# Block 0's in-projections: planning the products of three pairs of heads before the fourth pair's x is there

## The chip, the cores and the metric

The kernel runs on one core of a Trainium2 chip, with its TensorE (PE in the profile), VectorE (DVE), ScalarE (ACT), GpSimd (POOL) and the queue of SyncE (SP) that issues most of the DMAs. The metric is the device time of one execution in microseconds; the median of three runs of the kernel before is 1342.89 us.

## What is computed

Attention over 8 batches of 8 heads, 576 positions and 64 channels, in which every score below the row's maximum less tau is dropped, and then a gated unit (a GLU) over all 4608 tokens. The reference, cut:

```
scores = scale * (q @ k.T)
scores = where(scores >= max(scores) - tau, scores, -1e9)
attn   = exp(scores - max(scores)); attn /= sum(attn) + 1e-9
x      = (attn @ v)            # per token: 8 heads x 64 = 512 channels
gate   = 1 / (1 + exp(-(x @ w_gate)))      # 512 -> 1536
out    = (gate * (x @ w_val)) @ w_out      # 1536 -> 512
```

The gate's weights are drawn large, so the products are made with split operands: each float32 is a high and a low part, and a product is the sum of three matmuls (high x high, high x low, low x high).

## The kernel before

**Attention.** A `Visit` is one pair of heads of one batch: 4 visits a batch, 32 in all. A visit has 9 tiles of 128 queries. For each tile TensorE makes the scores (tile `s`, L653 in the first four visits, L661 after them), VectorE takes their maximum (L668), ScalarE the exponential (L682), VectorE cuts and sums (L685), TensorE transposes the result (tiles `tp`, `lk`, L767 and L780), ScalarE copies that to SBUF (`pt`, L718), and TensorE multiplies by v (`av`, L803). The result of a visit is `xf`. In three visits of four the division by the row sums comes late, on `xf`, by way of a small DMA round trip and a GpSimd multiply (`late_normalise`, L713); the visit of the fourth pair (`hp == 3`) divides before its transposes (L756).

**x.** `split_x` turns `xf` into `x`, with a high part by ScalarE (L813) and a low part by GpSimd (L815). The four pairs of a batch are the four 128-row pieces of the 512 channels of x.

**In-projections.** `in_units` handles a block of 512 tokens (here: blocks 0, 1 and 2; the others are worked two at a time by another function). For each of 12 pieces f of the 1536 columns and each of i = 0 (gate) and i = 1 (value), one sum is made in a PSUM bank `m`: 4 pairs c times 3 matmuls, twelve products (L863), in the order of c. They are given to the planner in twos. Twelve products with what follows are a unit. After a gate's sum ScalarE takes the tanh (`th`, L877); after a value's sum VectorE multiplies (L881), and the halves go to `g`. The first operation of a value's sum also reserves `g[f]` and `th`.

**Weights.** `convert` brings the weights from 64-bit pairs to high and low parts, with ScalarE (L487, L508), VectorE (L490, L496) and GpSimd (L483, L514). It is spread over attention. Its intermediate `wb` takes a PSUM bank from L487 to L496. The first 16 weights of the in-projections stay in buffers of `g` (at most ten of the twelve until these are needed), the next 8 in buffers of `w`; block 0 reads all 24 from there. A copy goes to DRAM (L519) for the later blocks.

**The planner.** Each piece of work is an operation with an engine, an estimated cost, a key, and the buffers that it reads and writes. `Plan.run` plays the whole kernel through with these costs. An engine that is free takes the ready operation with the smallest key whose buffers have room (`room`). The order so found is the order in which instructions are written out, and each engine works through its instructions in that order. On the chip an instruction waits for the data that it itself reads. Attention has keys of 0 to some 340, the products of the unit have keys from 1e6 on, in order: TensorE takes a product only where no operation of attention is ready and has room. From the second visit of batch 1 on, attention is held to the pace of the units (`held_by`).

**PSUM.** There are eight banks. Before the first product is given out, scores have three buffers of two banks each (0-1, 2-3, 4-5), and banks 6 and 7 serve everything else (`tp`, `lk`, `av` and the conversions' `wb`). The operation with key 1e6, the first product, switches that (`started`): scores keep two buffers, and banks 4 and 5 join 6 and 7 when they are free. While attention lasts, sums may hold two of these four, attention two and conversions one:

```
            if cls == "conv":
                return 1
            if cls == "att":
                return 2 if active["moe"] else 3
            return 2 if active["att"] else 4
```

The rule that the change touches is in `in_units`: which pairs of x an operation of two products (j and j + 1) is said to read.

```
cs = range(ND) if ms[j + step - 1][0] >= FIRST_PAIRS else range(FIRST_PAIRS)
```

`ms[e][0]` is the pair of product e (0 to 3), `step` is 2, and ND is 4.

Of the kernel before, what the change touches and what calls it, by code (L numbers as in the profile page):

```python
# [281 lines left out]
def LATE(b, hp):  # L282
    return hp != 3

FIRST_PAIRS = 4
KD_COST = 1.2

TWOS = ((3, 4), (5, 6), (7, 8))
# [27 lines left out]
def kernel(  # L316
# [528 lines left out]
    def in_units(blk, xs, g, c0, c1, c0x, weights):  # L845
# [5 lines left out]
        for f in [f + z for f in F1 for z in (0, 2)] if blk in SUMS_IN else range(NF):  # L851
            th = buf("t2", [P, W], F32, f"th{blk}_{f}_{c0}")
            for i in range(2):
# [4 lines left out]
                for j in range(0, 12, step):  # L858
# [9 lines left out]

                    cs = range(ND) if ms[j + step - 1][0] >= FIRST_PAIRS else range(FIRST_PAIRS)
                    xr = [xs[c] if part is None else (xs[c], (z, c0)) for c in cs for z in range(2)]  # L870
# [516 lines left out]
```

## Time and profile before

| | us |
|---|---|
| median of three runs | 1342.89 |
| fastest and slowest of them | 1341.32, 1348.61 |
| span of the profiled execution | 1340.2 |
| VectorE, ScalarE, GpSimd busy in it | 944.4, 727.8, 492.7 |
| first and last in-projection product of block 0 (L863, weights ws) | 98.1, 231.7 |
| first and last of blocks 1 and 2 (L863, weights wi) | 324.4, 766.4 |

The profile is of one execution, and its own time is given by its span, the time from the first to the last instruction. The runs' times also hold what lies around the span. The profile has views by stretch of time (busy time of each engine, number of instructions in brackets, granted TensorE clock, share and rate of DMA), timelines of single engines, and groups by line. In the latter, a row has the number of instructions, their shortest, median and longest duration in ns, and the first and last start in us. TensorE's weight loads are a row of their own (PEld) and run beside its matmuls.

### The profile page before, as it was taken

To read this page: it belongs to the slowest core of one execution; us is meant where nothing else is said; L and a number is where in the kernel's file an instruction comes from. 1 tells how busy PE (TensorE), PEld (TensorE's weight loads), DVE (VectorE), ACT (ScalarE), POOL (GpSimd) and SP (SyncE) were. 2 spreads that over 40 slices of the span, in tenths; PEclk is the share of its full clock that TensorE was granted. 3 is DMA by queue.
4 is the path that set the end of the run, shared out by engine and by line. 5 is a ranking of instruction groups with operands and counts; after the bars stand their busy time and mean duration, and the time that the engine had idled before them with its cause. 6 is when DMAs were issued, how large, how long until landed. Compare 5 with 4: busy or idle time off the path is not lost.

```text
span 1340.2 us, 23378 instructions
## 1 busy us (share of the span) xinstructions
PE 1314.8 (98%) x8292; PEld 1077.3 (80%) x8292; DVE 944.4 (70%) x1868; ACT 727.8 (54%) x1339; POOL 492.7 (37%) x474
## 2 busy tenths in 40 slices
PE   8889999999999999999999999999999999999998
PEld 5558887888888888888888888888888888888887
DVE  7888888777787776776777763556955569554594
ACT  8887777667767766666666652223522235322242
POOL 3576867724455363456464441110001010001100
PEclk9999999999999999999999999999999999999999
DMA  8889998999798888998988957656686566756563
GB/s 298 240 260 311 321 259 263 269 260 288 198 254 259 239 241 244 260 293 230 264 246 259 236 190 267 221 191 207 211 286 196 189 204 206 247 178 204 190 217 117
DMA packets 148115, 318.72 MB, mean 238 GB/s; under 512 B 28192, under 2 KB 56096, under 8 KB 148000
## 3 DMA queue, kind: packets, MB, share of 16 engines
q1 hardware_dynamic: 147856, 317.24, 78.3%
q8 instruction: 66, 1.08, 0.3%
q14 instruction: 49, 0.40, 0.1%
q10 hardware_dynamic: 144, 0.00, 0.0%
HBM read 211.16 MB, written 54.64 MB: 198 GB/s over the span
## 4 chain that ended last, share of the span: by engine, by line
PE 91%; DMA 4%; ACT 2%; POOL 1%; DVE 1%; issue 1%; SPq 0%; DVEq 0%; POOLq 0%; ACTq 0%
PE m L863 13%; PE qb L1105 11%; PE av L803 11%; PE s L661 8%; PE tp L767 8%; PE qc L1105 7%; PE qa L1105 7%; PE o L906 7%; PE rb L1170 5%; PE rc L1170 4%; PE ra L1170 4%; PE s_l L661 1%; PE tp_l L767 1%; PE s L653 1%; PE lk L780 1%
## 5 line engine op out<-in xcount | busy, mean ns | idle before, releaser
L668 DVE TENSOR_REDUCE st<-s 128x1 f32<-128x576 f32 x256 | 192.4, 753 | 83.2 <-PE s L661 76.0
L685 DVE SCALAR_TENSOR_TENSOR p<-s,st,p 128x576 f32<-128x576 f32 x256 | 206.5, 813 | 44.7 <-ACT p L682 39.4
L682 ACT ACTIVATE p<-s,st 128x576 f32<-128x576 f32 x256 | 191.1, 751 | 35.1 <-DVE st L668 34.4
L718 ACT COPY pt<-tp 128x512 f32<-128x512 f32 x256 | 149.4, 588 | 83.1 <-PE tp L767 79.1
L1018 POOL TENSOR_TENSOR gA<-gA 128x512 f32<-128x512 f32 x18 | 24.1, 1341 | 409.5 <-DVE gA L1084 409.5
L661 PE MATMUL s<-kd,qd 128*128 128x288 f32 x896 | 163.2, 306 | 2.6 <-DVE p_l L685 1.9
L863 PE MATMUL m<-x,wi 128*128 128x512 f32 x576 | 164.9, 405 | 0.0
L767 PE MATMUL tp<-ident,p 128*128 128x128 f32 x1024 | 155.4, 276 | 8.2 <-ACT pt L718 4.1
L767 PEld LDWEIGHTS tp<-ident,p 128*128 128x128 f32 x1024 | 119.8, 140 | 40.4 <-ACT pt L718 5.6
L661 PEld LDWEIGHTS s<-kd,qd 128*128 128x128 f32 x896 | 134.5, 189 | 13.4 <-DVE p_l L685 2.6
L803 PE MATMUL av<-pt,vs 128*64 128x256 f32 x1024 | 124.6, 385 | 0.8 <-ACT pt L718 0.8
L906 PE MATMUL o<-g,wo 128*128 128x512 f32 x432 | 120.4, 404 | 0.0
L1105 PE MATMUL qa<-xs_p,wa 128*128 128x512 f32 x432 | 109.4, 389 | 0.0
L1042 DVE TENSOR_TENSOR qu<-qb,qp 128x512 f32<-128x512 f32 x72 | 49.8, 692 | 82.5 <-PE qb L1105 71.2
L863 PEld LDWEIGHTS m<-x,wi 128*128 128x128 f32 x576 | 98.0, 189 | 12.0
L803 PEld LDWEIGHTS av<-pt,vs 128*64 128x64 f32 x1024 | 67.9, 136 | 48.5 <-issue 9.5
L1105 PEld LDWEIGHTS qa<-xs_p,wa 128*128 128x128 f32 x432 | 81.1, 188 | 16.8
L906 PEld LDWEIGHTS o<-g,wo 128*128 128x128 f32 x432 | 74.7, 189 | 10.0
L863 PE MATMUL m<-x,ws 128*128 128x512 f32 x288 | 78.5, 404 | 1.5 <-ACT pt L718 1.5
L887 POOL TENSOR_TENSOR g<-th,g 128x512 fp32r<-128x512 f32 x36 | 46.7, 1296 | 58.0 <-ACT g L885 57.8
L756 POOL TENSOR_SCALAR p<-p,zero_t,sm 128x576 f32<-128x576 f32 x64 | 56.5, 892 | 31.1 <-DVE sm L754 19.3
L1010 ACT CAST gs_p<-gA 128x512 fp32r<-128x512 f32 x54 | 32.8, 620 | 61.4 <-DVE gA L1084 23.0
(145 smaller groups left out, 2542.1 us busy)
## 6 DMA issues: line engine op xcount, KB each, us to landing
kd<-k SPq DMA_DIRECT2D x112, 320.0 KB
wi<-wid SPq DMA_DIRECT2D x48, 512.0 KB
wo<-wod SPq DMA_DIRECT2D x36, 512.0 KB
wa<-wid SPq DMA_DIRECT2D x36, 512.0 KB
ws<-sid SPq DMA_DIRECT2D x36, 512.0 KB
wt<-sid SPq DMA_DIRECT2D x36, 512.0 KB
wo_p<-sod SPq DMA_DIRECT2D x36, 512.0 KB
qd<-q SPq DMA_DIRECT2D x112, 128.0 KB
```

The costliest lines, as they stand in the source:

```text
L661: nc.tensor.matmul(s.ap[:, c, :HALF], st(), mv(slice(kc + c * HALF, kc + (c + 1) * HALF)), start=m == 0, stop=m == len(steps) - 1,)
L668: op("DVE", 0.76, key, lambda: nc.vector.tensor_reduce(out=st.ap[:, 0:1], in_=sv(), axis=AX.XY, op=ALU.max, negate=True), reads=[s], write ...
L682: op("ACT", 0.74, key, lambda: nc.scalar.activation(p(), sv(), AF.Exp, bias=st.ap[:, 0:1], scale=1.0), reads=[s, (st, 0)], writes=[(g.p, i)])
L685: op("DVE", 0.9, key, lambda: nc.vector.scalar_tensor_tensor(out=p(), in0=sv(), scalar=st.ap[:, 1:2], in1=p(), op0=ALU.is_ge, op1=ALU.mult ...
L718: return op("ACT", act(n), key, lambda: nc.scalar.copy(dst(), src.ap), reads=[src], writes=[part])
L756: op("POOL", 0.9, key, lambda i=i: nc.gpsimd.tensor_scalar(out=p.ap[:, i * S : (i + 1) * S], in0=p.ap[:, i * S : (i + 1) * S], scalar1=zer ...
L767: nc.tensor.matmul(tp.ap[:, c, :], self.p.ap[:, o + c * P : o + (c + 1) * P], ident, is_transpose=True, start=c == 0, stop=c == NJ - 1, sk ...
L803: nc.tensor.matmul(av.ap[h * D : (h + 1) * D, a:z], vis.vs.ap[:, j, h], m(h), start=i == 0, stop=i == len(ms) - 1, skip_group_check=True,)
L863: nc.tensor.matmul(m.ap, wv[:, a, c * P : (c + 1) * P], xs[c].ap[:, z, c0:c1], start=e == 0, stop=e == 11,)
L906: nc.tensor.matmul(acc.ap, wv[:, f, a], g[fg * ND + f].ap[:, z], start=(fg, f, a, z) == (0, 0, 0, 0), stop=(fg, f, a, z) == (NFG - 1, ND - ...
L1105: nc.tensor.matmul(acc.ap, wv[:, y, (2 * h + c) * P : (2 * h + c + 1) * P], xt[prod][c].get()[:, z], start=e == 0 and prod in FIRST, stop= ...
L1170: nc.tensor.matmul(acc.ap, w.ap[:, e, c, y], gt[prod][2 * g + c].get()[:, z], start=m == 0 and g == 0 and prod in FIRST, stop=m == 5 and g ...
```

## The change

One constant. With 4, every operation of two products is planned to read all four pairs of x. With 3, an operation whose later product belongs to one of the first three pairs is planned to read those three, and one whose later product belongs to the fourth is planned to read all four.

```diff
@@ -282,7 +282,7 @@
 def LATE(b, hp):
     return hp != 3
 
-FIRST_PAIRS = 4
+FIRST_PAIRS = 3
 KD_COST = 1.2
```

The instructions that are written out are the same; their order may differ.

## Prediction

> **What bounds the kernel now.** I read the page from the top: the shares of the engines, then the chain that ended last.
>
> ```profile
> span 1340.2 us, 23378 instructions
> PE 1314.8 (98%) x8292; PEld 1077.3 (80%) x8292; DVE 944.4 (70%) x1868; ACT 727.8 (54%) x1339; POOL 492.7 (37%) x474
> PE 91%; DMA 4%; ACT 2%; POOL 1%; DVE 1%; issue 1%; SPq 0%; DVEq 0%; POOLq 0%; ACTq 0%
> ```
>
> TensorE is busy for 1314.8 of 1340.2 us and is 91% of the last chain. An edit that leaves its matmuls as they are can only move the remaining 25.4 us. So the next view is the one that gives busy time by stretch, cut at the moments around the change: 79.84 (x of the third pair is complete), 98.13 (the first product of block 0 starts), 140, 800 (attention is over).
>
> ```profile
> core 0: us, PE busy (x) PEld busy (x) DVE busy (x) ACT busy (x) POOL busy (x), PEclk, DMA share, GB/s
> 0.00:79.84 79.84, 67.87 (x539) 43.04 (x540) 65.12 (x139) 65.75 (x125) 42.97 (x73) 1.00 0.81 266
> 79.84:98.13 18.29, 14.20 (x124) 10.21 (x122) 17.44 (x35) 15.85 (x31) 14.58 (x16) 1.00 0.84 256
> 98.13:140.00 41.87, 41.07 (x266) 33.88 (x267) 35.73 (x74) 32.17 (x62) 26.25 (x24) 1.00 1.02 306
> 140.00:800.00 660.00, 655.51 (x4969) 546.72 (x4968) 494.64 (x1125) 446.11 (x835) 355.46 (x324) 1.00 0.89 254
> 800.00:1325.00 525.00, 525.00 (x2353) 434.50 (x2352) 329.42 (x494) 167.88 (x289) 53.46 (x40) 1.00 0.65 212
> ```
>
> Idle TensorE time is length less busy time: 11.97 us before 79.84, then 4.09, 0.80, 4.49 and 0.00 us. From 98.13 on TensorE is the bound. In the 18.29 us before it is not: there VectorE is busy for 17.44 us. That stretch is the only place where the change can collect anything.
>
> Its two ends come from the timeline of GpSimd, whose L815 completes x of one pair, and its gaps from the timeline of TensorE (columns: start, length, what; in brackets the idle time before it).
>
> ```profile
> 78.57 1.27 POOL L815 TENSOR_TENSOR x<-xf,x 128x512 fp32r<-128x512 f32 x1
> 92.62 1.28 POOL L815 TENSOR_TENSOR x<-xf,x 128x512 fp32r<-128x512 f32 x1 [1.53 <-ACT x L813]
> ```
> ```profile
> 80.42 0.33 PE L780 MATMUL lk<-ident,p 128*128 128x128 f32 x1 [0.24 <-ACT pt L718]
> 81.01 0.78 PE L661 MATMUL s<-kd,qd 128*128 128x288 f32 x4 [0.26 <-DMA xp<-xf]
> ...
> 85.24 0.63 PE L767 MATMUL tp<-ident,p 128*128 128x128 f32 x4 [0.41 <-ACT xf L718]
> 86.63 0.63 PE L767 MATMUL tp<-ident,p 128*128 128x128 f32 x4 [0.77 <-ACT pt L718]
> ...
> 87.72 0.80 PE L661 MATMUL s<-kd,qd 128*128 128x288 f32 x4 [0.35 <-DVE p L685]
> ...
> 94.61 0.66 PE L767 MATMUL tp_l<-ident,p_l 128*128 128x128 f32 x4 [0.57 <-ACT pt L718]
> ...
> 96.80 0.65 PE L767 MATMUL tp<-ident,p 128*128 128x128 f32 x4 [0.65 <-ACT pl_l L718]
> 98.13 3.02 PE L863 MATMUL m<-x,ws 128*128 128x512 f32 x12 [0.68 <-ACT pt L718]
> ```
>
> x of the third pair is complete at 78.57 + 1.27 = 79.84 us, x of the fourth at 93.90 us, and the first product starts at 98.13 us. The eight gaps shown sum to 3.93 us.
>
> **The change, part by part.** It removes and adds no instruction. It changes one list of reads that the planner goes by. Products are planned in twos, and a two waits for all four pairs as soon as its second product belongs to the fourth. So of the twelve products of a sum the first eight, four twos, can go after the third pair; the ninth shares a two with the tenth and still waits. The rule stands for blocks 1 and 2 too, but there x is early:
>
> ```profile
> L863 PE MATMUL m<-x,wi x576: 387/393/486, 324.4 to 766.4; 128*128 128x512 f32 x192
> ...
> L815 POOL TENSOR_TENSOR x<-xf,x x4: 1279/1286/1290, 145.9 to 235.3; 128x512 fp32r<-128x512 f32 x4
> ```
>
> Block 1 multiplies from 324.4 us; its last x was split at 235.3 us. Nothing to win or lose there, and block 2's x is reloaded in the same way during the work before it. The first weights are not late either: their copies go out from 30.7 us on.
>
> ```profile
> L519 SPq DMA_DIRECT2D wid<-ws x11: 321/343/782, 30.7 to 104.0; - x11
> ```
>
> *How much can move.* Two sums may be open beside attention (the cap of two banks), so 2 x 8 = 16 products. Twelve took 3.02 us at 98.13, 0.252 us each: 16 x 0.252 = **4.03 us** of TensorE work. The stretch has 4.09 us idle, so it would just fit. It issues no DMA: weights of block 0 lie in SBUF. Nothing on SP's or GpSimd's queue is passed.
>
> *What of it lands in gaps.* A sum needs a PSUM bank, and until the first product has been given out, attention and weight conversion share two. So I let the first product start some us after 79.84 and count the gaps from 86.63 on: 0.77 + 0.35 + 0.57 + 0.65 + 0.68 = 3.02 us. Bounds: 0 (no bank, or the order doesn't change) and 4.03 us. I take **3.4 us**, between 3.02 and 3.93, the gaps from 80.42.
>
> *What it costs.* TensorE works in order, so a two (0.50 us) that has begun holds up scores and transposes behind it, and with them VectorE, which has only 18.29 - 17.44 = 0.85 us to spare, and so x of the fourth pair. Also, with the first product the planner takes the third scores buffer from attention and gives its two banks to the others. Both together are in the trace, in the next stretch (L685 has two records a tile):
>
> ```profile
> 79.84:98.13 18.29, 4.83 (x12) 1.00 0.84 256
> 98.13:140.00 41.87, 9.70 (x24) 1.00 1.02 306
> ```
> ```profile
> 98.13:140.00 41.87, 26.79 (x104) 18.52 (x104) 1.00 1.02 306
> ```
>
> The first fence is L685, the second the products of L863. Before 98.13 a tile takes 18.29 / 6 = 3.05 us, after it 41.87 / 12 = 3.49 us, with products on TensorE for 26.79 / 41.87 = 64% of the time. At worst the six tiles get that slower pace: 6 x 0.44 = 2.6 us. But the moved products are only 4.03 / 18.29 = 22% of the stretch, so I scale: 2.6 x 22 / 64 = **0.9 us**. Bounds 0 and 2.6. The second sum also reserves its output g and th at its first product; as the early weights are kept to ten of the twelve g buffers, one conversion may slip. It is off TensorE, and I cost it at nothing; were it on the chain, it would cost its place there, about 3 us (below).
>
> *Sum.* 3.4 - 0.9 = 2.5 us less. On the profiled span: 1340.2 - 2.5 = 1337.7 us. The median run, 1342.89, lies 2.7 us above the span (the fastest, 1341.32, 1.1 us), so I forecast 1342.9 - 2.5 = **1340.4 us**.
>
> [...]
>
> **The rivals.**
>
> *A. Nothing is collected.* The first product finds no free bank until about where it is now, or the delay of x eats the gain (3.0 - 2.6 = 0.4 us). For it: x of the fourth pair is ready at 93.90, yet the first product starts 4.23 us later. Against it: the gaps at 85 to 88 us are waits for a copy or for VectorE, in which the planner had nothing else to give to TensorE. Time: 1342.9 us less 0 to 0.4.
>
> *B. Slower: open sums sit on the banks.* The two half sums can't finish before the fourth pair's x, 14.06 us after the third's. If they take the two banks that attention and conversion use, these have to live on the pair that the third scores buffer leaves. While that buffer is still held, or if only one of the pair serves, conversion and transposes take turns. A conversion's hold on its bank:
>
> ```profile
> 83.63 0.66 ACT L487 ACTIVATE wb<-wr 128x512 f32<-128x512 f32 x1
> ```
> ```profile
> 86.25 0.69 DVE L496 SCALAR_TENSOR_TENSOR wa<-wr,wb 128x512 int32<-128x512 int32 x1
> 86.85 0.81 DVE L685 SCALAR_TENSOR_TENSOR p<-s,st,p 128x576 f32<-128x576 f32 x1
> ```
> ```profile
> 79.84:98.13 18.29, 3.27 (x5) 1.00 0.84 256
> ```
>
> That is 86.94 - 83.63 = 3.3 us, five times in the stretch (last fence, L487). Each conversion that attention has to sit out costs 3.3 us; the point from which B decides is one. A scores buffer can be held for 6.6 us (scores at 81.01, consumed at 87.66, the L685 above), so two may fall into the hand-over: 2 x 3.3 - 3.4 = 3.2 us slower, **1346 us**; all five, 13.1 us slower, 1356 us. The half of the sums that takes the freed pair instead speaks against it: then attention and conversion have two banks, as before.
> [...]
>
> *C. The order after it is dealt anew.* All of attention to 800 us is placed by the same planner, so a moved start moves everything behind it. From 98.13 to 800 TensorE idles 0.80 + 4.49 = 5.3 us. Another order can save all of that or double it: 1340.4 - 5.3 = 1335.1 to 1340.4 + 5.3 = 1345.7 us. From 800 to 1325 there is no idle time to change.
>
> **How the numbers follow.** Forecast 0.45 (alone: 1338.9, if all 4.03 us are won, to 1342.5), A 0.20, B 0.17, C 0.18. About 0.5%, 6.7 us, is what a measurement of this kernel can tell from no change; the three runs before spread over 7.3 us. Faster by more than that, below 1336.2, only the lucky end of C reaches, helped by the spread of runs: 0.09. Slower by more, above 1349.6: B from three conversions on, and the spread on top of C: 0.15. Within: 0.76. The range runs from C's lucky end, 1335, to 1349, between B's two conversions and its three (1342.9 + 9.9 - 3.4 = 1349.4).
>
> **What would show it.** Right: L863's first start falls from 98.1 to 80 to 88 us, with 16 products ahead of the fourth x split; idle TensorE time between 79.84 and some 99 us falls from 4.09 to under 2 us; the fourth x split ends at 93.9 to 96.5 us. A: first start above 93 us, or the split late by as much as was filled. B: longer gaps before tp and lk, with releasers of pt, wb or wa, and the split after 97 us. C: an unlike idle time from 98 to 800 us than 5.3. The forecast is wrong if TensorE waits in order for a product whose x isn't there, which would show as a gap ahead of L863 released by L815.

## The result and the profile after

The changed kernel takes 1354.51 us (median of 6 runs, 1349.72 to 1358.86) against 1343.55 us before (6 runs, 1341.32 to 1348.61). The ratio is 1.0078, with a 95% interval of 1.0053 to 1.0103: slower by 11.0 us, where 2.5 us less were forecast. The measured time lies above the range.

The page of the profile after, with the same rows as before:

```profile
span 1353.3 us, 23378 instructions
PE 1321.2 (98%) x8292; PEld 1078.2 (80%) x8292; DVE 944.6 (70%) x1868; ACT 727.2 (54%) x1339; POOL 494.5 (37%) x474
PE 88%; DMA 5%; ACT 2%; SPq 1%; POOL 1%; DVE 1%; issue 1%; ACTq 0%; POOLq 0%; DVEq 0%
```

The third row above carries the shares of the chain that ended last. The span is 13.1 us longer. Idle TensorE time is 1353.3 - 1321.2 = 32.1 us, 6.7 more than before; busy time is 6.4 us more, for the same 8292 matmuls. So there are two losses to find: gaps, and matmuls that take longer.

Busy time by stretch, cut where it was cut before:

```profile
0.00:79.84 79.84, 68.87 (x532) 43.27 (x532) 65.00 (x139) 64.58 (x122) 41.35 (x71) 0.98 0.81 264
79.84:98.13 18.29, 16.05 (x131) 12.25 (x131) 15.83 (x31) 14.06 (x28) 11.74 (x13) 1.00 0.75 218
98.13:140.00 41.87, 41.09 (x262) 34.09 (x263) 37.00 (x71) 35.00 (x68) 32.86 (x30) 1.00 0.99 328
140.00:800.00 660.00, 646.32 (x4888) 535.17 (x4887) 481.81 (x1105) 438.38 (x824) 345.37 (x313) 0.99 0.88 250
800.00:1325.00 525.00, 524.43 (x2377) 433.50 (x2376) 334.31 (x508) 170.72 (x295) 63.18 (x49) 1.00 0.65 213
```

In the stretch at which the change aims, idle TensorE time fell from 4.09 to 2.24 us. From 140 to 800 us it rose from 4.49 to 13.68 us. Nothing of the changed line runs there in a new way: blocks 1 and 2 had their x early.

The start of the products, in TensorE's timeline, and x of the third and fourth pair, in GpSimd's:

```profile
82.31 2.11 PE L863 MATMUL m<-x,ws 128*128 128x512 f32 x8 [0.16 <-ACT pt L718]
```
```profile
79.97 1.27 POOL L815 TENSOR_TENSOR x<-xf,x 128x512 fp32r<-128x512 f32 x1
96.58 1.29 POOL L815 TENSOR_TENSOR x<-xf,x 128x512 fp32r<-128x512 f32 x1 [6.26 <-ACT x L813]
```

The first product starts at 82.31 instead of 98.13 us. x of the fourth pair is complete at 97.87 instead of 93.90 us.

**Where the time goes.** Two stalls between 200 and 260 us. Each is a chain over several engines, so it is shown by one row of each engine's timeline. The first, from SP's, ScalarE's and TensorE's timeline:

```profile
205.11 1.05 SPq L523 DMA_DIRECT2D wod<-ws  x1
```
```profile
212.61 0.62 ACT L508 CAST ws<-wa 128x512 fp32r<-128x512 f32 x1 [4.76 <-DMA wod<-ws]
```
```profile
213.77 3.00 PE L803 MATMUL av<-pt,vs 128*64 128x256 f32 x16 [2.49 <-ACT pt L718]
216.55 1.07 PE L803 MATMUL av<-pl,vs 128*64 128x128 f32 x8
217.56 0.89 PE L863 MATMUL m<-x,ws 128*128 128x512 f32 x2
```

A converted weight `ws` is to go into a `w` buffer whose old content is on its way to DRAM (L523). ScalarE stands for 4.76 us until the store that SP issued at 205.11 us has landed, 7.4 us after it. Behind that instruction stand the copy of `pt` and two exponentials, and TensorE waits for the copy. The second stall, in the same order with GpSimd's timeline added:

```profile
232.57 0.56 SPq L989 DMA_DIRECT2D sod<-s_o  x1
233.42 0.55 SPq L1278 DMA_DIRECT2D xp<-xf  x1
234.06 1.20 SPq L989 DMA_DIRECT2D sod<-s_o  x1
235.31 6.86 SPq L841 DMA_DIRECT2D wo<-wod  x3
```
```profile
241.16 1.27 POOL L957 TENSOR_TENSOR s_o<-wo 128x512 f32<-128x512 f32 x1 [10.48 <-DMA sod<-s_o]
```
```profile
249.01 0.62 ACT L968 CAST s_o<-s_o 128x512 fp32r<-128x512 f32 x1 [4.45 <-POOL s_o L957]
249.53 0.58 ACT L718 COPY pt<-tp 128x512 f32<-128x512 f32 x1
```
```profile
245.58 0.63 PE L906 MATMUL o<-g,wo 128*128 128x512 f32 x2
250.17 1.12 PE L767 MATMUL tp<-ident,p 128*128 128x128 f32 x4 [3.96 <-ACT pt L718]
250.94 2.06 PE L906 MATMUL o<-g,wo 128*128 128x512 f32 x4
```

GpSimd prepares sums of output weights for the blocks that are worked two at a time (`out_sums`), in `w` buffers too. The next such sum waits 10.48 us for a buffer that is still being stored: by L989 at 232.57 us, and this store lands at 241.03 us. SP itself waits 5.2 us for the second store, the one of 234.06 us; the last of its three loads stands behind that, so the row of 6.86 us is mostly waiting (`SPq L841 <- DMA sod<-s_o: 5.2, 1, 5.2` in the view of SP's waits). Behind GpSimd's waiting instruction stand the low parts of two x and one g and four more steps of the sum; ScalarE's next step waits for those, the copy of `pt` stands behind that, and TensorE idles for 3.96 us. TensorE's releaser reads "ACT pt" in both stalls, but it is neither ScalarE nor its copy: one has to follow the queue back to the store.

After each gap the matmuls are slow: sixteen `av` take 3.00 us where the same group takes 1.95 us elsewhere in both timelines, and four `o` take 2.06 instead of 1.09 us (at 235.30). The granted clock, in the view by stretch (the column after the five engines), says why. The first row is that of the first stall:

```profile
210.00:220.00 10.00, 7.51 (x46) 5.31 (x45) 3.98 (x9) 4.17 (x9) 7.12 (x7) 0.83 0.98 362
240.00:250.00 10.00, 5.29 (x45) 3.87 (x41) 3.23 (x8) 2.59 (x5) 8.03 (x9) 0.93 0.44 153
250.00:260.00 10.00, 9.83 (x74) 7.48 (x75) 4.75 (x9) 6.19 (x13) 9.06 (x9) 0.73 0.36 112
```

### The profile page after: what moved, and what is told of

It reads as the page before. It is cut to its first block, busy times and chain, and to the rows that moved or that the text cites. A ratio compares the mean times of both kernels' runs of the same rounds, so it can differ in the third digit from the quotient of the medians.

```text
span 1353.3 us, 23378 instructions
## 1 busy us (share of the span) xinstructions
PE 1321.2 (98%) x8292; PEld 1078.2 (80%) x8292; DVE 944.6 (70%) x1868; ACT 727.2 (54%) x1339; POOL 494.5 (37%) x474
## 4 chain that ended last, share of the span: by engine, by line
PE 88%; DMA 5%; ACT 2%; SPq 1%; POOL 1%; DVE 1%; issue 1%; ACTq 0%; POOLq 0%; DVEq 0%
PE m L863 13%; PE av L803 11%; PE qb L1105 11%; PE s L661 8%; PE tp L767 7%; PE qa L1105 7%; PE qc L1105 7%; PE o L906 6%; PE rb L1170 5%; PE rc L1170 4%; PE ra L1170 4%; PE s_l L661 1%; PE s L653 1%; DMA kd<-k 1%; PE tp_l L767 1%
## 5 line engine op out<-in xcount | busy, mean ns | idle before, releaser
L580 POOL TENSOR_TENSOR k<-kn,k 128x640 fp32r<-128x640 f32 x28 | 43.6, 1556 | 72.7 <-ACT k L576 48.1
```

## Experiments

Three theories stood against each other. Theory 1: the loss is waits for `w` buffers that are still being stored. Theory 2: the early sums cost by themselves (rival B: banks, the third scores buffer). Theory 3: any new order of the planner's costs or gains like this, and the early products bring only their small gain. Theories 1 and 3 can both hold: 1 says what the loss is, 3 why it came up.

**A tenth w buffer, the order unchanged.** The planner still counts nine, so each engine has the same instructions in the same order; the chip has ten buffers to put them in. The pad and some small buffers make room. The same edit was made to both kernels.

```diff
-    cp.tile([P, PAD], F32, tag="pad", name="pad")
...
     slots = {t: n for t, (_, n) in pools.items()}
+    pools["w"], pools["st"], pools["sm"] = (sb, 10), (sb, 8), (sb, 4)
```

The changed kernel with it:

> Changed kernel with the same order on every engine, but ten buffers behind the tag w on the chip instead of nine (the planner still counts nine; the unused pad goes, st and sm get 8 and 4 buffers to make room). Theory 1, the loss is waits for w buffers whose old content is still on its way to DRAM: the two stalls at 208 to 214 and 246 to 250 us shrink, idle TensorE time in 200 to 260 us falls from about 9 to under 4 us, and the time from 1354 to 1342 to 1348 us. Theory 2, the early sums themselves cost (banks, third scores buffer): the time stays at 1351 to 1357 us.

The kernel before with it:

> The same tenth buffer in the kernel before. Theory 1: no wait of that kind stops TensorE there, so 1340 to 1345 us, within 3 us of the kernel before. If it gains as much as the changed kernel does (5 us or more), the tenth buffer is a gain of its own and says nothing of the change.

And the changed kernel with the pad gone and the small buffers small, but nine w buffers:

> Control for the tenth buffer: changed kernel, order the same, w still with nine buffers, but without the pad and with 8 and 4 buffers for st and sm as in the run with ten. Theory 1 (waits for w buffers): 1351 to 1357 us, the two stalls between 200 and 260 us are back. If it comes out at 1341 to 1347 us, the pad or the small buffers made the difference, not w.

| | us (runs) | ratio to the kernel before, 95% |
|---|---|---|
| changed, ten w | 1344.4 (10) | 1.0004, 0.9989 to 1.0019 |
| before, ten w | 1345.06 (10) | 1.0009, 0.9988 to 1.0031 |
| changed, nine w, rest as with ten | 1355.93 (4) | 1.0088, 1.0065 to 1.0111 |

Theory 1 holds: one buffer more takes 1354.51 - 1344.4 = 10.1 of the 11.0 us away, does nothing for the kernel before (1345.06 us, just above the 1345 that were expected), and the pad and the small buffers have no part in it. Theory 2 falls: the early sums and the banks that they hold are the same in the first and the third row. The waits for DMAs between 195 and 260 us (who waited for whom; total, times, longest), first with nine buffers and the small ones small, then with ten:

```profile
POOL s_o L957 <- DMA sod<-s_o: 10.3, 1, 10.3
ACT ws L508 <- DMA wod<-ws: 5.0, 1, 5.0
```
```profile
ACT ws L508 <- DMA wod<-ws: 2.4, 1, 2.4
ACT xf L718 <- DMA wo<-wod: 1.2, 1, 1.2
```

GpSimd's wait for `sod` is gone and ScalarE's for `wod` is half as long. TensorE from 200 to 325 us, the changed kernel with nine, then with ten:

```profile
200.00:325.00 125.00, 113.75 (x815) 91.70 (x815) 80.74 (x189) 74.78 (x143) 62.89 (x59) 0.96 0.85 242
```
```profile
200.00:325.00 125.00, 122.44 (x936) 100.84 (x935) 90.79 (x206) 84.99 (x164) 74.65 (x69) 1.00 0.94 272
```

Idle time falls from 11.25 to 2.56 us and the clock is back at 1.00. Busy TensorE time over the span is 1317.0 us with ten buffers against 1321.2, so at least about 4.2 us of the loss were matmuls at a lower clock (at least, because the profile with ten had the lower clock for longer at its start, 0.87 against 0.91 over the first 20 us).

**New orders without and with the early products.** Four numbers with which the planner reckons were moved by a little, in both kernels. Each gives another order; only in the changed kernel do products start early.

```diff
-LAG = {"PE": 1.0, "DVE": 0.3, "ACT": 0.08, "POOL": 0.3, "SP": 0.08}
+LAG = {"PE": 1.05, "DVE": 0.3, "ACT": 0.08, "POOL": 0.3, "SP": 0.08}
```

> Kernel before with one planner number moved by a little: TensorE's assumed lag 1.05 us instead of 1.0. The order is dealt anew, no product starts early. Theory 3, the loss is the lot of a new order: anywhere from 1338 to 1358 us, likely slower than 1343 by some us. If orders cost alike: 1341 to 1346 us.

> Changed kernel with the same moved number. Theory 2, the early sums cost: 8 to 14 us above the kernel before with that number. Theory 3, the lot of the order: the difference to it may have either sign, and the early products themselves bring 2 to 4 us less idle TensorE time before 140 us.

The second pair has 0.95 for TensorE:

> Kernel before with TensorE's assumed lag at 0.95 us instead of 1.0: another order, no early products. Theory 3 (the lot of the order): 1338 to 1356 us.

> Changed kernel with the same number. Theory 2 (the early sums cost): 8 to 14 us above its partner. Theory 3: the difference to its partner has either sign and lies within 12 us; idle TensorE time from 20 to 200 us is 2 to 3 us less than its partner's.

The third has 0.1 for ScalarE:

> Kernel before with ScalarE's assumed lag at 0.10 us instead of 0.08: another order, no early products. Theory 3: 1338 to 1356 us.

> Changed kernel with the same number. Theory 2: 8 to 14 us above its partner. Theory 3: the difference has either sign and lies within 12 us; idle TensorE time from 20 to 200 us is 2 to 3 us less than its partner's.

The fourth lets DMAs land later:

```diff
-                        done = dma + 3.0
+                        done = dma + 4.5
```

> Kernel before, with the planner taking a DMA as landed 4.5 us after its transfer instead of 3.0, nearer to the 7.4 us from issue to landing that the store at 205 us took. The order is dealt anew and buffers are planned for reuse later. Theory 3 (the lot of the order): 1338 to 1356 us. If too early reuse costs the kernel before as well: 1338 to 1342 us.

> Changed kernel with the same later landing. Theory 1: no engine waits long for a store of a w buffer between 200 and 260 us, so idle TensorE time there is under 4 us and the time 1338 to 1346 us. Theory 2 (the early sums cost): 8 to 14 us above the kernel before with the same number. Theory 3: either sign, with 2 to 3 us less idle TensorE time between 20 and 200 us.

Times with their ratios to runs of the kernel before that were made along with them (95% intervals in brackets), and idle TensorE time from 20 to 200 us, that is 180 us less the busy time of the one profile of each:

| planner | no early products, us | early products, us | difference | idle 20 to 200, without and with |
|---|---|---|---|---|
| as it was | 1343.55 | 1354.51, 1.0078 (1.0053 to 1.0103) | +11.0 | 12.1, 9.6 |
| lag of PE 1.05 | 1350.06, 1.0042 (1.0023 to 1.0060) | 1339.92, 0.9970 (0.9951 to 0.9989) | -10.1 | 11.5, 9.5 |
| lag of PE 0.95 | 1347.06, 1.0027 (1.0011 to 1.0042) | 1343.79, 1.0004 (0.9988 to 1.0021) | -3.3 | 13.3, 9.5 |
| lag of ACT 0.10 | 1342.22, 0.9989 (0.9972 to 1.0006) | 1351.02, 1.0060 (1.0041 to 1.0079) | +8.8 | 11.8, 13.3 |
| landing 4.5 | 1353.27, 1.0070 (1.0044 to 1.0095) | 1343.83, 1.0006 (0.9990 to 1.0022) | -9.4 | 20.0, 11.7 |

The rows behind the last column, as it was before the change, after it, and with the lag of 1.05 and early products:

```profile
20.00:200.00 180.00, 167.87 (x1256) 126.67 (x1257) 154.40 (x322) 144.22 (x276) 119.08 (x129) 1.00 0.91 276
```
```profile
20.00:200.00 180.00, 170.42 (x1267) 129.24 (x1268) 157.09 (x318) 145.52 (x277) 120.45 (x131) 1.00 0.88 274
```
```profile
20.00:200.00 180.00, 170.47 (x1256) 128.30 (x1257) 153.71 (x315) 143.34 (x272) 114.88 (x127) 0.99 0.88 272
```

The first half of theory 3 holds: a new order alone moves the time by as much as the change did. Without any early product the time runs from 1342.2 to 1353.3 us, with them from 1339.9 to 1354.5 us. The difference has both signs, twice plus and three times minus, and its mean over the five pairs is -0.6 us; five pairs can't tell that from nothing, and they do not give the change a sign. That the early products bring their small gain, the second half, these times can't show; it rests on the idle times. Theory 2's 8 to 14 us appear in one new pair of four.

The expected 2 to 3 us less idle time before 200 us came in none of the three pairs for which it was named: it was 3.8 us less with the lag of 0.95, 8.3 us less with the later landing, and 1.5 us more with ScalarE's lag. (For the lag of 1.05, 2 to 4 us less before 140 us were expected; from 20 to 140 us it is 1.9 us.) The pair with ScalarE's lag is the weakest evidence: both profiles are of the slowest run of their kernel (1349.66 and 1356.59 us), and TensorE's clock was lowered in part of the stretch in both, to 0.97 and 0.98 over the 180 us; slower matmuls, like the sixteen `av` above with 3.00 instead of 1.95 us, make busy time out of idle time. Why the sign is the other way there stays open. The later landing did for the changed kernel what theory 1 asked of it: no engine waits there for the store of a w buffer, and TensorE has no idle time from 200 to 260 us:

```profile
200.00:260.00 60.00, 60.00 (x448) 50.24 (x447) 44.74 (x98) 43.45 (x84) 41.69 (x37) 1.00 0.87 248
```

But it is no safer rule for orders: without early products the same number lost 20.0 us in gaps ahead of 200 us.

**Is it always the w buffers?** The changed kernel with ScalarE's lag at 0.10 is slow as well. It got the tenth buffer too, by the edit shown above:

> Changed kernel with ScalarE's assumed lag at 0.10 us (1351.0 us) and, with the same order on every engine, the tenth w buffer. If early products always run into waits for w buffers: 1341 to 1346 us, as in the changed kernel. If each order has a stall of its own, and this one's is elsewhere (its profile has a wait of 4.6 us for VectorE after 325 us and no long wait for a w buffer before): 1348 to 1354 us, as without the tenth buffer.

It takes 1349.3 us (10 runs), ratio 1.0056 (1.0025 to 1.0087), against 1351.0 us with nine buffers. So its loss lies elsewhere, as far as w buffers go. The longest wait of TensorE after 325 us, with nine and then with ten buffers:

```profile
PE s L661 <- DVE p_l L685: 4.6, 1, 4.6
```
```profile
PE s L661 <- DVE p_l L685: 4.4, 1, 4.4
```

Behind that wait stands one VectorE instruction, L583, which took 7.24 us (7.10 with ten buffers); the last section returns to it.

```profile
418.89 7.24 DVE L583 SCALAR_TENSOR_TENSOR q<-qn,scale_t,q 128x640 fp32r<-128x640 f32 x1 [0.78 <-ACT q L578]
```

So these two orders have different stalls. Stalls can also recur: with the lag of 0.95 and early products ScalarE again waits 5.0 us at L508 for a store of a `w` buffer, and TensorE idles for 2.67 us at 211.41 us. TensorE has no second stall in that order, which takes 1343.79 us.

## Why the prediction was wrong

**What moves: right.** With the rule set to three for piece f = 0 of block 0 alone, every engine's instructions stand in the same order as in the changed kernel; with it set for blocks 1 and 2 alone, they stand as before. Sixteen products moved, eight of each of two sums, between 82.31 and 98.0 us, in the window of 80 to 88 us that was given for the first. Two of the other signs did not come as given: idle time in the stretch fell to 2.24 us and not to under 2, and the fourth x split ended at 97.87 us and not by 96.5.

**The gain: right in size, partly by luck.** The sum was 3.4 us filled less 0.9 us lost, 2.5 us. In the stretch itself idle time fell by 4.09 - 2.24 = 1.85 us. From 20 to 200 us TensorE idles 12.13 - 9.58 = 2.55 us less; the other profiles of the same two orders have 12.5 us before and 9.5 and 10.1 us after, so 2.0 to 3.0 us. The filled gaps and the delay were not measured apart, so that the sum came out at 2.5 is in part luck. The price in delay was larger than taken: x of the fourth pair came 97.87 - 93.90 = 3.97 us later, of which 1.40 us were there already at the third pair's (79.97 against 78.57 us), so 2.57 us, the upper bound of 2.6 and not 0.9. That cost no idle time, since TensorE had the other work of attention to do. By idle time four of the five pairs gain before 200 us. The forecast's mechanism is there in the pair that was predicted, and is as small as it was said to be.

**Rival A** did not come about: the bank was free at 82.31 us.

**Rival B** had the right sign for the wrong reason. It put the loss where sums hold banks, at 80 to 98 us; gaps there shrank, and with the same sums and one more w buffer the loss was gone. One of its signs appeared all the same: the split came after 97 us, but 1.40 us of that were there before any product moved.

**Rival C is the step that failed**: "Another order can save all of that or double it". The sum of 2.5 us has no term at all for what happens behind 98 us; that was left to C. C sized a new order by the idle time that the old one had left from 98.13 to 800 us, 5.3 us, and made it even on both sides. Measured, that idle time went to 0.78 + 13.68 = 14.5 us, nearly three times. Two things were overlooked. The old order's idle time says how well one order fits, not how badly another can: in the second stall GpSimd's wait for a store took ScalarE, TensorE and VectorE with it. And idle time was taken as the only lever, though both gaps were followed by a lower clock, which cost about 4.2 us of busy time. The prediction also put a late conversion at nothing because it is off TensorE; at 212 us one did hold TensorE, since ScalarE, which ran it, had the copy of `pt` behind it. C deserved more than 0.18 and a range from some 4 us faster to 11 us slower than the kernel before, which is what the nine new orders show (ratios 0.9970 to 1.0078). A range of 1335 to 1349 us was too narrow for that reason alone.

**Where the waits come from, and what stays open.** The kernel's code shows more than the runs alone. The planner's `room` counts how many of the nine `w` buffers are in use; when an instruction is written out, `make` asks the pool for one of them, and which one the pool gives is not planned. Played through with the planner's own times, the changed kernel has three places before 260 us where the buffer that is given is one whose store the planner itself still has on its way, though another buffer was free: for the weight of L508 by 4.5 us, for the sum of L957 by 8.4 us, and for a load on SP by 4.9 us. These are the three waits of the trace, 4.76, 10.48 and 5.2 us, for the same stores. With the tenth buffer ScalarE's place is left with 1.9 us, and the wait there was 2.4 us. The kernel before has three such places too, but all on loads of SP. It is not that the planner reckons these stores too short: it has the first two on their way for 15.6 and 12.2 us from issue to landing, where the chip took 7.4 and 8.5 us, so the 7.4 us were no reason for a later landing. No run gives another of the nine buffers with all else held, so that this is the cause is read from the code and the trace, and not tested.

How the 10 us divide between the two stalls is open as well: the tenth buffer eased both at once. The changed order with the lag of 0.95 has a first stall alone and is no slower than the kernel before, which points at the second, but all of its order is new. With the later landing these waits are gone from the changed kernel, but there too the whole order is new.

## What to carry to other kernels

Where a planner makes the order of all engines from assumed costs, a local edit is two edits: its own, which can be read from the stretch (here 2 to 3 us of idle time), and a new draw of the order for all that follows (here from 4 us faster to 11 us slower than the kernel before); price the second by a few neutral nudges of the planner, with and without the edit, before the edit is believed or dropped. A buffer too many on the chip, with the order held, tells a wait for a buffer from other causes, once a control has what else had to change for it. And a planner that counts buffers should also say which one is given. The draw with a lag of 1.05 and early products is the fastest here, 0.9970 (0.9951 to 0.9989) of the kernel before, but it is a draw and no rule.

## What was not expected of the hardware

A gap of 1.91 us was followed by a lower clock. In the kernel before, it is TensorE's longest wait behind 200 us, and the two products after the gap take 0.90 us instead of the 0.63 us that two take at 227.12 us:

```profile
219.60 0.80 PE L661 MATMUL s<-kd,qd 128*128 128x288 f32 x4 [1.91 <-DVE p_l L685]
220.24 0.90 PE L863 MATMUL m<-x,ws 128*128 128x512 f32 x2
```
```profile
220.00:230.00 10.00, 10.00 (x54) 8.69 (x53) 7.00 (x16) 5.74 (x12) 6.23 (x7) 0.83 0.94 245
```

Not every such gap is. In the kernel before with a lag of 1.05 TensorE idles for 2.44 us up to 213.55 us, and the clock behind it stays at 1.00:

```profile
213.55 0.33 PE L780 MATMUL lk<-ident,p 128*128 128x128 f32 x1 [2.44 <-ACT pt L718]
```
```profile
213.00:223.00 10.00, 9.45 (x66) 6.93 (x68) 7.49 (x14) 8.44 (x18) 8.25 (x7) 1.00 1.06 364
```

After the changed kernel's gaps of 2.49 and 3.96 us the clock was 0.83 (210 to 220 us) and 0.73 (250 to 260 us). So the length of a gap does not tell by itself whether a lower clock follows: 1.91 us had one behind it, 2.44 us had none.

The gap of 1.91 us itself came from one VectorE instruction (L583) that took 5.18 us, with a median of 1.45 us over its 28. The traces show what goes with such a length. GpSimd worked without a pause from before L583's start to 216.80 us, and L583 ended 0.68 us later:

```profile
212.30 5.18 DVE L583 SCALAR_TENSOR_TENSOR q<-qn,scale_t,q 128x640 fp32r<-128x640 f32 x1
```
```profile
215.49 1.31 POOL L957 TENSOR_TENSOR s_o<-wo 128x512 f32<-128x512 f32 x1
219.60 1.29 POOL L514 TENSOR_TENSOR ws<-wa,ws 128x512 fp32r<-128x512 f32 x1 [2.80 <-ACT ws L508]
```

The L583 of 7.24 us in the changed kernel with ScalarE's lag is alike: GpSimd pauses for 0.08 us at 425.45 us, and L583 ends at 426.13 us, again 0.68 us later. In all profiles of this case L583 runs 392 times; the 44 that meet no GpSimd instruction take 0.87 to 0.89 us each. All that take over 2 us have GpSimd at work beside them for most of that time: in the profiles before and after the change these are four, of 2.08 to 5.18 us, with GpSimd at work for 87% or more of each. No run moves GpSimd's work away and leaves the rest, so the pause and the end that follows it are seen three times (the 7.10 us with ten buffers are the third), but as a cause this was not tested.

The start differs from run to run: the first twelve score matmuls took 1.82 us in the profile before and 2.28 us in the one after, with a clock of 1.00 and 0.91 over the first 20 us (0.91 as well in the kernel before with ten buffers, which has the order of the first). At 59 us that had made 1.4 us of difference between the two profiles, ahead of anything that the change touches.
